# A gated mix of softmax and linear attention on one core: changed order of work, ten P slots, more zero-adding matmuls

## The chip, the cores and the metric

One NeuronCore of a Trainium2 chip runs the whole kernel in one launch. The metric is the device time in microseconds (us); lower is better. Four engines matter: PE (TensorE, matmuls), ACT (ScalarE, the exponentials), DVE (VectorE) and, at the edges, POOL (GpSimd). Transfers are issued by SP and ACT.

## The reference, cut to what matters

```python
x = A_x                                   # [1, 2048, 512] bf16
g = sigmoid((x * gate_w).sum(-1, keepdims=True))
# A: softmax attention, 32 heads of width 16
q, k, v = heads(x @ A_wqkv)
a = merge(softmax(q @ k.T * 16 ** -0.5) @ v) @ A_wo
# B: linear attention, 32 heads of width 16
q, k, v = heads(x @ B_wqkv)
phi = lambda t: where(t > 0, t + 1, exp(t)) + 1e-6
pq, pk = phi(q), phi(k)
b = merge((pq @ (pk.T @ v)) / (pq @ pk.sum(0) + 1e-6)) @ B_wo
return g * a + (1 - g) * b
```

Nearly all of the work is in `softmax(q @ k.T) @ v`: 32 heads of 2048 x 2048 scores, each of which needs an exponential.

## The kernel before, in words

**Rounds.** The attention is cut into 32 rounds (`NR`): a round is one chunk of 512 queries and four heads, one for each quarter of the PE rows. A round has 16 key blocks of 128 keys; a key block has four units, one per head, each a 128 x 512 tile of transposed scores.

**The ACT path.** `emit_act_group` (L809) issues the score matmuls of three or two units, in turn, into PSUM banks 0 to 2 or 3 and 4 (they use 32 rows of PE each and run side by side), and then one exponential on ACT (L826) that reads these banks and writes one slot of `PT`. There are `NPT` = 7 slots. `emit_pv` (L876) multiplies four units of a key block by V into the accumulator, bank 7 (four matmuls with 17 columns each, side by side); a slot is free again when its units have been used. Score matmuls have to wait until ACT has read their banks, and ACT has to wait for a free slot.

**The DVE path.** Of a round's key blocks, the last ones (11 to 15) may be claimed for DVE (`d_claim`, L922). For such a block PE makes the scores one unit at a time in a spare bank, 5 or 6 (`emit_d`, or riding with an ACT group, `d_ride`); DVE turns each into 16-bit integers in `Lb` (`d_s1`, L1002), and a chain of four instructions over the whole block (`chain_op`: L1024, L1027, L1031, L1034) makes two factors `Eb` and `Xb` out of the bits. `emit_dpv` then takes three passes of PE, with `Lb`, `Eb` and `Xb`, into the accumulator. A block of the next round may be claimed ahead of time, as far as the buffers go (three of `Lb` and `Xb`, `NE` = 2 of `Eb`); its passes wait until the accumulator is at its round. For the current round a block is claimed only while

```python
if max(DV.clock, PE.clock) + DLAT > AC.clock + rem * 0.445 + DGRACE:
    continue
```

is false, with `DLAT, DGRACE = 10.5, 2.0` and `rem` the units that the round still has for ACT.

**The end of a round.** When every unit of the round is in the accumulator, `round_end` (L896) transposes it on DVE (L899) and scales it. The next round's PV matmuls need the same bank and wait for L899.

**Everything else** (projections, casts of K, Q and V, the linear attention, the output projection) is cut into tasks, generators that yield one PE or DVE step at a time, in banks 5 and 6. Each task has a due time, by which the tasks are sorted, and a time before which it doesn't start (`nb`), both in rounds. What a round needs and hasn't got is finished on the spot (`need`). V comes in two parts: `V0` for the first eight heads, and `V1`, one task per key block, for the other 24, which are first used in the third round. POOL makes `VX`, a scaled copy of V for blocks 11 to 15.

**The order** is laid out when the program is built. A loop (from L1123 on) keeps a clock for each engine from fixed costs, collects the candidates (0 ACT group, 1 DVE scores, 2 PV, 3 DVE passes, 4 tasks, 5 a chain instruction), and of those that are ready takes the one with the lowest number that ends before the next ACT group has to be issued (`must`). What it emits is each engine's queue, in this order for good. Where nothing fits and the gap on its own clock is long enough, it emits a dummy (`emit_dummy`): four matmuls of zeros, 17 columns each, added to the accumulator, if the accumulator is free by its clock and if the columns that it lately sent through PE (`warm_count`) are under `WARMC`:

```python
if gap > mcost("col", 1) - 0.05 and warm_count() < WARMC and dummy_cand() <= now and apos[0] < NR:
    emit_dummy()
    continue
```

All matmuls are recorded under one helper, L358; tiles tell them apart (scores `sb_QP,sb_KT`, PV `sb_PT,sb_V`, dummies `sb_warm`).

Of the kernel before, what the change touches and what calls it, by code (L numbers as in the profile page):

```python
# [13 lines left out]

STATS = {}
LOG = []
INF = 1e18
SEMLAT = 0.05

# [106 lines left out]
def _ready(E, reads, writes):  # L126
    t = 0.0
    for d in _deps_for(E, reads, writes):
        if d is not None:
            t = max(t, d.t)  # L130
    return t
# [14 lines left out]
def bass_gated_mix__mha_block__linear_attn_block__prompt_kernel(  # L146
# [14 lines left out]
    NTB = S // 128  # L161
# [1 line left out]
    NCC = D // 128  # L163
    SCALE = float(Dh) ** -0.5
    NR = NQC * 8
    NPT = 7
    NL = 3
    NE = 2
    NX = 3
    DKB0 = 11  # L170
    VW = Dh + 1

    with ExitStack() as es:
# [118 lines left out]
        def op(E, fn, reads=(), writes=(), cost=0.2):  # L292
            ev = E.add(fn, _deps_for(E, reads, writes), cost=cost, lag=0.12 if E is AC else 0.0)
            _record(E, ev, reads, writes)
            return ev
# [37 lines left out]
        def mcost(m, waves):  # L333
            return (0.0 if m == mode[0] else 0.095) + 0.015 + 0.2145 * waves

        def pe(fns, reads=(), writes=(), waves=1.0, m="full", cols=None):
            deps = _deps_for(PE, reads, writes)
            n = len(fns)
            first = None
            cost = mcost(m, waves)  # L340
            mode[0] = m
            for k, fn in enumerate(fns):
                ev = PE.add(fn, deps if k == 0 else (), inc=(k == n - 1), cost=cost / n, lag=0.155)
                if k == 0:
                    first = ev
            first.t = ev.t
            c = 512.0 * waves if cols is None else cols
            hist.append((PE.clock, c))
            hsum[0] += c
            for res in reads:  # L350
                res.r[PE] = first
            for res in writes:
                res.w = ev
                res.r = {}
            return ev

        def mm(o, l, r, start=True, stop=True, sg=False):
            return lambda: nc.tensor.matmul(o, lhsT=l, rhs=r, start=start, stop=stop, skip_group_check=sg)  # L358
# [297 lines left out]
        bykey = {}  # L656
        MISCB = [6, 5]
        maxhold = [2]
        DLAT, DGRACE = 10.5, 2.0
        WARMC = 3550.0  # L660

        def add(key, gen, due, nb=-1.0, pre=()):
            t = Task()
            t.pre = list(pre)
            t.key, t.gen, t.due, t.nb, t.seq = key, gen, due, nb, len(bykey)
            t.bank, t.done, t.started = None, False, False
            t.req = next(gen)
            tasks.append(t)
            bykey[key] = t
            tasks.sort(key=lambda k: (k.due, k.seq))  # L670
# [214 lines left out]
            pv_left[r] -= 4  # L885
            round_check()

        def dummy_cand():
            return _ready(PE, (), [r_acc]) + SEMLAT

        def emit_dummy():
            STATS["dummies"] = STATS.get("dummies", 0) + 1
            pe([mm(acc[32 * j:32 * j + VW, :], warm[:, 0:VW], warm, start=False, stop=False, sg=True) for j in range(4)],
               reads=[r_warm], writes=[r_acc], waves=1, m="col", cols=512)

        def round_end(r):  # L896
            qc, t8, par = rinfo(r)
# [24 lines left out]
        def d_claim():  # L922
            r = apos[0]
            if r >= NR or progress() < 0.8:
                return None
            for rr in (r, r + 1):
                if rr >= NR or rr < 1:
                    continue
                kb = NTB - 1 - claimed[rr]
                if kb < DKB0 or act_done[rr]:  # L930
                    continue
                if kb - front[rr] < 1:
                    continue
                if rr == r:
                    rem = 4 * (NTB - claimed[rr] - 1) - apos[1]
                    if max(DV.clock, PE.clock) + DLAT > AC.clock + rem * 0.445 + DGRACE:
                        continue
                return rr, kb
            return None
# [27 lines left out]
        def d_bank():  # L967
            free = [b for b in MISCB if b not in held]
            if not free:
                return None  # L970
            return min(free, key=bank_free)
# [8 lines left out]
            return b, rd, ready  # L980

        def d_ride(js):
            if not d_start() or d_bank() is None:
                return None
            b, rd, ready = d_ready()
            if max(ready, DV.clock - 1.3) > PE.clock + 0.02:
                return None
            for j in dst["cur"]["js"]:
                if j not in js:
                    return j, b, rd  # L990
            return None

        def d_cand():
            if not d_start() or d_bank() is None:
                return None
            b, rd, ready = d_ready()
            return max(ready, DV.clock - 0.5), b, rd

        def d_s1(j, b):
            cu = dst["cur"]  # L1000
            sl = cu["ls"]
            ev = op(DV, lambda: nc.vector.tensor_scalar(Lb[:, sl, 512 * j:512 * (j + 1)], BK[b], S1A, S1B, op0=ALU.mult, op1=ALU.add),  # L1002
                    reads=[r_bk[b]], writes=[r_L[sl]], cost=0.691)
            cu["js"].remove(j)
            if not cu["js"]:
                cu["rdy"][0] = ev.t
                chainq.append(cu)
                dst["cur"] = None
# [66 lines left out]
                add(("Q", 0, 0), t_qproj(0, 0), -0.19, pre=[("xtr", 0)])  # L1075
            add(("V0", t), t_v0(t), 0.25 * t - 0.15, pre=[("xtr", t)])
        for tb in range(NTB):
            add(("V1", tb), t_v1(tb), 1.2 + 0.05 * tb, 0.5 + 0.08 * tb, pre=XT)
        for tb in range(DKB0, NTB):
            add(("VX0", tb), t_vx(0, tb), 0.8, 0.7, pre=[("V0", tb // 4)])  # L1080
            add(("VX1", tb), t_vx(1, tb), 1.9, 1.5, pre=[("V1", tb)])
        add(("gate",), t_gate(), 0.6, 0.5, pre=XT)
        for t8 in range(1, 4):
            for t in range(4):
# [37 lines left out]
        while True:  # L1122
# [21 lines left out]
            if cx is not None:  # L1144
                cands.append((cx[0], 3, mcost("col", 1), emit_dpv, cx))
            for (rt, kind, t, waves) in misc_candidates():
                cands.append((rt, 4, mcost("full", waves) if kind == "pe" else 0.0, lambda c: advance(c[0]), (t,)))
            if chainq:
                cands.append((max(now, DV.clock - 0.3), 5, 0.0, chain_op, None))
            if not cands:  # L1150
                if not tasks and apos[0] >= NR and not pvq and not dpv:
                    break
# [2 lines left out]
                        t.nb = -1  # L1155
                    continue
                raise AssertionError(("stuck", apos, acc_round, len(pvq), [t.key for t in tasks][:5]))
            avail = sorted((c for c in cands if c[0] <= now + 0.02), key=lambda c: c[1])
            pick = None
            for c in avail:  # L1160
                if c[1] == 0 or c[2] == 0.0 or now + c[2] <= must:
# [2 lines left out]
            if pick is None:  # L1164
                pick = cands[0] if avail and act_live else min(cands, key=lambda c: c[0])
                gap = pick[0] - now
                if gap > mcost("col", 1) - 0.05 and warm_count() < WARMC and dummy_cand() <= now and apos[0] < NR:
                    emit_dummy()
                    continue
                if PE.clock < pick[0] < INF:  # L1170
                    PE.clock = pick[0]
# [66 lines left out]
```

## Time and profile before

| | before |
|---|---|
| median of 2 runs | 933.72 us (928.06 and 939.39) |
| profiled execution | 930.83 us, of which the span of the instructions is 929.0 us |
| mean granted TensorE clock | 0.838 |
| ACT busy | 809.3 us (87%) |
| PE busy | 801.4 us (86%) |
| DVE busy | 670.8 us (72%) |
| key blocks taken by DVE | 82 (instructions of L1024) |
| dummies among the rounds | 588 matmuls, in fours 147 |

Two runs 11 us apart are all that the median rests on. In the rows below, a group of instructions reads: line, engine, operation, output<-inputs, shapes, count | busy time in us, mean ns of one | idle time of the engine just before them, and what ended it. A line of the timeline reads: start, duration, engine, line, operation, count, and in brackets the idle time before it and what ended it. A line of a table by stretches reads: the stretch, its length, then busy us and count of instructions for PE, PEld, DVE, ACT and POOL, the granted TensorE clock (1.00 is 2.4 GHz, 0.50 is 1.2 GHz), the DMA share and GB/s; where a tile is chosen, of the instructions of that tile alone, and only the engines that have any. In a row of waits stand the total in us, how often, and the longest.

### The profile page before, as it was taken

The page shows a single profiled execution, that of the slowest core. Times are in us where ns is not written, and L with a number is a line of the kernel's source. Part 1 is how long each engine was busy: PE and PEld are TensorE (multiplying, and loading weights), DVE is VectorE, ACT ScalarE, POOL GpSimd, SP SyncE. Part 2 cuts the span into 40 slices and gives each one's busy share as a digit, 9 for nine tenths or more (in the row PEclk, how much of TensorE's full clock was granted, in tenths as well). Part 3 has the DMA queues.
Part 4 walks back from the last instruction along what each step waited for, and adds up shares of the span by engine and source line. Part 5 has one row for each costly group of instructions (what it writes and reads, how often), then busy time and mean ns, then how long its engine had stood idle before and what let it go on. Part 6 is the DMA issues. An engine that isn't in the chain of part 4 may idle for free.

```text
span 929.0 us, 14661 instructions
## 1 busy us (share of the span) xinstructions
PE 801.4 (86%) x6228; PEld 203.3 (22%) x6228; DVE 670.8 (72%) x1001; ACT 809.3 (87%) x723; POOL 16.6 (2%) x43
## 2 busy tenths in 40 slices
PE   5897898888888889898988888988898979988898
PEld 2322222211121112222112222222222222222112
DVE  3257778878777877856657888768667767878983
ACT  3995989999898978989978999979997979979994
POOL 2103000000000000000000000000000000000000
PEclk9989889979687867789757999997788789977856
DMA  9000000000000000101001000000000000000000
GB/s 215 1 7 1 7 1 5 2 1 7 1 7 1 3 5 1 30 1 52 1 1 52 1 7 9 23 22 1 18 24 12 11 16 26 7 8 18 6 1 23
DMA packets 30769, 14.72 MB, mean 16 GB/s; under 512 B 18544, under 2 KB 30704, under 8 KB 30704
## 3 DMA queue, kind: packets, MB, share of 16 engines
q1 hardware_dynamic: 26512, 11.95, 4.9%
q10 hardware_dynamic: 4192, 1.84, 1.0%
q8 instruction: 49, 0.80, 0.3%
q14 instruction: 16, 0.13, 0.0%
HBM read 6.55 MB, written 2.10 MB: 9 GB/s over the span
## 4 chain that ended last, share of the span: by engine, by line
ACT 56%; PE 34%; DVE 7%; issue 2%; DMA 1%; ACTq 0%; DVEq 0%
ACT sb_PT L826 54%; PE ps L358 34%; DVE sb_Lb L1002 2%; ACT sb_ebuf L528 1%; DMA sb_OT<-in_A_wqkv_dram 1%; DVE sb_Xb L1034 1%; DVE sb_Xb L1031 1%; DVE sb_U L899 1%; DVE sb_Eb L1027 0%; DVE sb_wA L646 0%; DVE sb_xnat L532 0%; DVE sb_Xb L1024 0%; DVE sb_ebuf L530 0%; DVE sb_V L495 0%; DVE sb_phiK L532 0%
## 5 line engine op out<-in xcount | busy, mean ns | idle before, releaser
L826 ACT ACTIVATE sb_PT<-ps 128x1536 bf16<-128x1536 f32 (+1 forms) x688 | 796.9, 1306 | 93.9 <-PE ps L358 91.9
L358 PE MATMUL ps<-sb_QP,sb_KT 32*128 32x512 bf16 x2048 | 357.6, 444 | 84.5 <-ACT sb_PT L826 73.6
L1002 DVE TENSOR_SCALAR sb_Lb<-ps 128x512 uint16<-128x512 f32 x328 | 222.3, 688 | 162.1 <-PE ps L358 160.7
L358 PE MATMUL ps<-sb_PT,sb_V 128*17 128x512 bf16 x1720 | 192.6, 449 | 10.1 <-DVE sb_U L899 8.5
L358 PEld LDWEIGHTS ps<-sb_QP,sb_KT 32*128 32x128 bf16 x2048 | 79.1, 93 | 381.8 <-ACT sb_PT L826 263.1
L1034 DVE TENSOR_TENSOR sb_Xb<-sb_Xb,sb_Lb 128x2048 bf16<-128x2048 bf16 x82 | 100.3, 1223 | 2.4
L1031 DVE TENSOR_TENSOR sb_Xb<-sb_Xb 128x2048 bf16<-128x2048 bf16 x82 | 99.8, 1217 | 0.0
L358 PEld LDWEIGHTS ps<-sb_PT,sb_V 128*17 128x17 bf16 x1720 | 40.7, 89 | 143.9 <-issue 120.0
L358 PE MATMUL ps<-sb_warm 128*17 128x512 bf16 (+1 forms) x596 | 63.9, 466 | 1.3 <-POOL sb_dummy L382 1.3
L1027 DVE TENSOR_SCALAR sb_Eb<-sb_Lb 128x2048 uint16<-128x2048 uint16 x82 | 56.2, 685 | 0.0
L1024 DVE TENSOR_SCALAR sb_Xb<-sb_Lb 128x2048 uint16<-128x2048 uint16 x82 | 56.0, 683 | 0.0
L358 PE MATMUL ps<-sb_Xb,sb_VX 128*17 128x512 bf16 x328 | 38.0, 453 | 11.1 <-DVE sb_Xb L1034 10.9
L358 PE MATMUL ps<-sb_Lb,sb_V 128*17 128x512 bf16 x328 | 39.1, 473 | 6.0 <-DVE sb_Lb L1002 5.2
L358 PE MATMUL ps<-sb_Eb,sb_V 128*17 128x512 bf16 x328 | 38.0, 453 | 2.4 <-DVE sb_Eb L1027 2.2
L358 PE MATMUL ps<-sb_xT,sb_wA 128*128 128x512 bf16 x108 | 31.4, 398 | 0.7 <-DVE sb_Lb L1002 0.5
L899 DVE STREAM_TRANSPOSE sb_U<-ps 128x512 f32<-128x512 f32 x32 | 22.7, 710 | 11.2 <-PE ps L358 10.5
L358 PE MATMUL ps<-sb_wBx,sb_xT 128*128 128x512 bf16 x64 | 24.9, 492 | 0.0
L528 ACT ACTIVATE sb_ebuf<-ps 128x512 f32<-128x512 f32 x32 | 21.4, 669 | 3.0 <-PE ps L358 3.0
L446 DVE CAST sb_KT<-ps 128x512 bf16<-128x512 f32 x16 | 11.0, 688 | 18.0 <-PE ps L358 17.9
L358 PE MATMUL ps<-sb_phiK,sb_xnat 128*128 128x512 bf16 x64 | 22.6, 458 | 0.2 <-DVE sb_Lb L1002 0.2
L646 DVE CAST sb_wA<-ps 128x512 bf16<-128x512 f32 x16 | 10.9, 688 | 16.1 <-PE ps L358 16.1
L358 PE MATMUL ps<-sb_phiK 128*128 128x512 bf16 x64 | 21.5, 439 | 0.0
(78 smaller groups left out, 324.7 us busy)
## 6 DMA issues: line engine op xcount, KB each, us to landing
out_dram<-sb_wA SPq DMA_DIRECT2D x16, 128.0 KB, 1.7
sb_QP<-sb_QT SPq DMA_DIRECT2D x120, 16.0 KB, 1.8
sb_xnat<-in_A_x_dram ACTq DMA_DIRECT2D x2, 512.0 KB, 5.6
sb_wA<-in_A_wqkv_dram SPq DMA_DIRECT2D x2, 512.0 KB, 7.0
sb_wBx<-in_B_wqkv_dram SPq DMA_DIRECT2D x2, 512.0 KB, 6.0
sb_xnat<-in_A_x_dram SPq DMA_DIRECT2D x2, 512.0 KB, 4.0
sb_phiK<-sb_wA SPq DMA_TRANSPOSE x64, 2.2
sb_wA<-in_A_wqkv_dram ACTq DMA_DIRECT2D x1, 512.0 KB, 5.8
```

The costliest lines, as they stand in the source:

```text
L358: return lambda: nc.tensor.matmul(o, lhsT=l, rhs=r, start=start, stop=stop, skip_group_check=sg)
L446: op(DV, lambda: nc.vector.tensor_copy(KT[:, t8, 512 * t:512 * (t + 1)], BK[b]), reads=[r_bk[b]], writes=[r_KT[t8][t]], cost=0.69)
L528: op(AC, lambda: nc.scalar.activation(ebuf[:, s, :], BK[b], ACT.Exp), reads=[r_bk[b]], writes=[r_e[s]], cost=0.68)
L646: op(DV, lambda: nc.vector.tensor_copy(outt[:, sl, :], BK[b]), reads=[r_bk[b]], writes=[r_outt[sl], r_wA[2]], cost=0.69)
L826: op(AC, lambda: nc.scalar.activation(PT[:, slot, 0:512 * n], ps[:, 512 * set_[0]:512 * (set_[0] + n)], ACT.Exp, scale=SCALE), reads=wr, w ...
L899: op(DV, lambda: nc.vector.transpose(U[:], acc), reads=[r_acc], writes=[r_U], cost=0.69)
L1002: ev = op(DV, lambda: nc.vector.tensor_scalar(Lb[:, sl, 512 * j:512 * (j + 1)], BK[b], S1A, S1B, op0=ALU.mult, op1=ALU.add), reads=[r_bk[b ...
L1024: ev = op(DV, lambda: nc.vector.tensor_scalar(X, L, 0x7F, 0x3F80, op0=ALU.bitwise_and, op1=ALU.bitwise_or), reads=[rl], writes=[rx], cost= ...
L1027: ev = op(DV, lambda: nc.vector.tensor_scalar(E_, L, 0xFF80, None, op0=ALU.bitwise_and), reads=[rl], writes=[re_], cost=CH[1])
L1031: ev = op(DV, lambda: nc.vector.tensor_tensor(xb, xb, xb, ALU.mult), reads=[rx], writes=[rx], cost=CH[2])
L1034: ev = op(DV, lambda: nc.vector.tensor_tensor(xb, xb, lb, ALU.mult), reads=[rx, rl], writes=[rx], cost=CH[3])
```

## The change: what it does

- **Claims.** `DLAT` is now a factor of 1.3 on the DVE work still ahead (the chains in the queue, 2.8 for the block's scores and 3.8 for its chain, in the planner's costs), and `DGRACE` is 4.0. With an empty queue the allowance is 1.3 x 6.6 - 4.0 = 4.6 where it was 10.5 - 2.0 = 8.5; with a whole chain in the queue it is 9.5. `NE` is 3.
- **A round's last block first.** `d_urgent` is true when the block at the head of the chain queue belongs to a round that ACT has left or is about to leave. Then no scores of a later round's block are started, and the chain is offered earlier. Chain instructions now rank ahead of the paid PE work (0.5 or 0.6 in place of 5), DVE steps of tasks ahead of everything (-1), and `d_s1` puts a chain instruction ahead of a score conversion for which DVE would have to wait.
- **P slots.** `NPT` is 10.
- **Like with like.** Among what is ready, PE work in the mode PE is in (row, column, full) comes first.
- **Zero-adding matmuls.** `WARMC` is 5200. `warm_mm` takes the place of `emit_dummy`; where the accumulator isn't free by the planner's clock (a round's end), it sends one full-size matmul of zeros to a free spare bank.
- **V1** goes from key block 15 down to 0 and starts and falls due earlier; `VX1` likewise.

A list for statistics (`COLS`) costs the chip nothing and is left out here.

```diff
--- before.py
+++ after.py
@@ -163,9 +164,9 @@
     NCC = D // 128
     SCALE = float(Dh) ** -0.5
     NR = NQC * 8
-    NPT = 7
+    NPT = 10
     NL = 3
-    NE = 2
+    NE = 3
     NX = 3
     DKB0 = 11
     VW = Dh + 1
@@ -656,8 +658,8 @@
         bykey = {}
         MISCB = [6, 5]
         maxhold = [2]
-        DLAT, DGRACE = 10.5, 2.0
-        WARMC = 3550.0
+        DLAT, DGRACE = 1.3, 4.0
+        WARMC = 5200.0
 
         def add(key, gen, due, nb=-1.0, pre=()):
             t = Task()
@@ -885,13 +887,20 @@
             pv_left[r] -= 4
             round_check()
 
-        def dummy_cand():
-            return _ready(PE, (), [r_acc]) + SEMLAT
-
-        def emit_dummy():
-            STATS["dummies"] = STATS.get("dummies", 0) + 1
-            pe([mm(acc[32 * j:32 * j + VW, :], warm[:, 0:VW], warm, start=False, stop=False, sg=True) for j in range(4)],
-               reads=[r_warm], writes=[r_acc], waves=1, m="col", cols=512)
+        def warm_mm(gap):
+            if apos[0] >= NR or warm_count() >= WARMC:
+                return False
+            now = PE.clock
+            if gap > mcost("col", 1) - 0.05 and _ready(PE, (), [r_acc]) + SEMLAT <= now:
+                pe([mm(acc[32 * j:32 * j + VW, :], warm[:, 0:VW], warm, start=False, stop=False, sg=True) for j in range(4)],
+                   reads=[r_warm], writes=[r_acc], waves=1, m="col", cols=512)
+                return True
+            if gap > mcost("full", 1) - 0.05:
+                for b in MISCB:
+                    if b not in held and bank_free(b) + SEMLAT <= now:
+                        pe([mm(BK[b], warm[:, 0:128], warm)], reads=[r_warm], writes=[r_bk[b]], waves=1)
+                        return True
+            return False
 
         def round_end(r):
             qc, t8, par = rinfo(r)
@@ -933,7 +942,8 @@
                     continue
                 if rr == r:
                     rem = 4 * (NTB - claimed[rr] - 1) - apos[1]
-                    if max(DV.clock, PE.clock) + DLAT > AC.clock + rem * 0.445 + DGRACE:
+                    back = sum(sum(CH[c["ck"]:]) for c in chainq) + 2.8 + sum(CH)
+                    if max(DV.clock, PE.clock) + DLAT * back > AC.clock + rem * 0.445 + DGRACE:
                         continue
                 return rr, kb
             return None
@@ -980,6 +990,8 @@
             return b, rd, ready
 
         def d_ride(js):
+            if d_urgent() and (dst["cur"] is None or dst["cur"]["r"] > chainq[0]["r"]):
+                return None
             if not d_start() or d_bank() is None:
                 return None
             b, rd, ready = d_ready()
@@ -990,7 +1002,15 @@
                     return j, b, rd
             return None
 
+        def d_urgent():
+            if not chainq:
+                return False
+            r = chainq[0]["r"]
+            return r < apos[0] or (4 * (NTB - claimed[r]) - apos[1]) * 0.445 + AC.clock < PE.clock + 6.0
+
         def d_cand():
+            if d_urgent() and (dst["cur"] is None or dst["cur"]["r"] > chainq[0]["r"]):
+                return None
             if not d_start() or d_bank() is None:
                 return None
             b, rd, ready = d_ready()
@@ -999,6 +1019,8 @@
         def d_s1(j, b):
             cu = dst["cur"]
             sl = cu["ls"]
+            if chainq and DV.clock < r_bk[b].w.t - 0.1:
+                chain_op()
             ev = op(DV, lambda: nc.vector.tensor_scalar(Lb[:, sl, 512 * j:512 * (j + 1)], BK[b], S1A, S1B, op0=ALU.mult, op1=ALU.add),
                     reads=[r_bk[b]], writes=[r_L[sl]], cost=0.691)
             cu["js"].remove(j)
@@ -1075,10 +1097,10 @@
                 add(("Q", 0, 0), t_qproj(0, 0), -0.19, pre=[("xtr", 0)])
             add(("V0", t), t_v0(t), 0.25 * t - 0.15, pre=[("xtr", t)])
         for tb in range(NTB):
-            add(("V1", tb), t_v1(tb), 1.2 + 0.05 * tb, 0.5 + 0.08 * tb, pre=XT)
+            add(("V1", tb), t_v1(tb), 0.9 + 0.05 * (15 - tb), 0.45 + 0.06 * (15 - tb), pre=XT)
         for tb in range(DKB0, NTB):
             add(("VX0", tb), t_vx(0, tb), 0.8, 0.7, pre=[("V0", tb // 4)])
-            add(("VX1", tb), t_vx(1, tb), 1.9, 1.5, pre=[("V1", tb)])
+            add(("VX1", tb), t_vx(1, tb), 1.7 - 0.1 * (tb - DKB0), 0.5, pre=[("V1", tb)])
         add(("gate",), t_gate(), 0.6, 0.5, pre=XT)
         for t8 in range(1, 4):
             for t in range(4):
@@ -1144,9 +1166,12 @@
             if cx is not None:
                 cands.append((cx[0], 3, mcost("col", 1), emit_dpv, cx))
             for (rt, kind, t, waves) in misc_candidates():
-                cands.append((rt, 4, mcost("full", waves) if kind == "pe" else 0.0, lambda c: advance(c[0]), (t,)))
+                cands.append((rt, 4 if kind == "pe" else -1, mcost("full", waves) if kind == "pe" else 0.0, lambda c: advance(c[0]), (t,)))
             if chainq:
-                cands.append((max(now, DV.clock - 0.3), 5, 0.0, chain_op, None))
+                if d_urgent():
+                    cands.append((max(now, DV.clock - 1.0), 0.5, 0.0, chain_op, None))
+                else:
+                    cands.append((max(now, DV.clock - 0.3), 0.6, 0.0, chain_op, None))
             if not cands:
                 if not tasks and apos[0] >= NR and not pvq and not dpv:
                     break
@@ -1155,7 +1180,9 @@
                         t.nb = -1
                     continue
                 raise AssertionError(("stuck", apos, acc_round, len(pvq), [t.key for t in tasks][:5]))
-            avail = sorted((c for c in cands if c[0] <= now + 0.02), key=lambda c: c[1])
+            pmode = {0: "row", 1: "row", 2: "col", 3: "col", 4: "full"}
+            avail = sorted((c for c in cands if c[0] <= now + 0.02),
+                           key=lambda c: (c[1] > 0 and c[2] > 0, c[1] if c[1] <= 0.6 else 1 if pmode[c[1]] == mode[0] else 2, c[1]))
             pick = None
             for c in avail:
                 if c[1] == 0 or c[2] == 0.0 or now + c[2] <= must:
@@ -1164,8 +1191,7 @@
             if pick is None:
                 pick = cands[0] if avail and act_live else min(cands, key=lambda c: c[0])
                 gap = pick[0] - now
-                if gap > mcost("col", 1) - 0.05 and warm_count() < WARMC and dummy_cand() <= now and apos[0] < NR:
-                    emit_dummy()
+                if warm_mm(gap):
                     continue
                 if PE.clock < pick[0] < INF:
                     PE.clock = pick[0]
```

## Rows read from the trace of the kernel before

**Rows 1.** The page, parts 1 and 2: busy time, granted clock in 40 slices.

```profile
PE 801.4 (86%) x6228; PEld 203.3 (22%) x6228; DVE 670.8 (72%) x1001; ACT 809.3 (87%) x723; POOL 16.6 (2%) x43
...
PEclk9989889979687867789757999997788789977856
```

**Rows 2.** The page, part 4: the chain that ended last, by engine.

```profile
ACT 56%; PE 34%; DVE 7%; issue 2%; DMA 1%; ACTq 0%; DVEq 0%
```

**Rows 3.** Waits, whole span: who waited for whom.

```profile
DVE sb_Lb L1002 <- PE ps L358: 160.7, 188, 4.3
ACT sb_PT L826 <- PE ps L358: 91.9, 88, 11.7
```

**Rows 4.** Groups by line, whole span.

```profile
L826 ACT ACTIVATE sb_PT<-ps 128x1536 bf16<-128x1536 f32 (+1 forms) x688 | 796.9, 1306 | 93.9 <-PE ps L358 91.9
...
L1002 DVE TENSOR_SCALAR sb_Lb<-ps 128x512 uint16<-128x512 f32 x328 | 222.3, 688 | 162.1 <-PE ps L358 160.7
...
L1034 DVE TENSOR_TENSOR sb_Xb<-sb_Xb,sb_Lb 128x2048 bf16<-128x2048 bf16 x82 | 100.3, 1223 | 2.4
...
L1024 DVE TENSOR_SCALAR sb_Xb<-sb_Lb 128x2048 uint16<-128x2048 uint16 x82 | 56.0, 683 | 0.0
```

**Rows 5.** Table of the 33 stretches at the lower granted clock: one, and their sum.

```profile
729.40:749.90 20.50, 20.50 (x146) 4.92 (x146) 12.67 (x19) 17.60 (x15) 0.00 (x0) 0.50 0.05 10
...
sum 300.20, PE 289.56 PEld 56.30 DVE 196.53 ACT 238.10 POOL 2.57; mean PE 8.77 PEld 1.71 DVE 5.96 ACT 7.22 POOL 0.08
```

**Rows 6.** Table of the 34 stretches at the upper granted clock: their sum.

```profile
sum 612.80, PE 503.73 PEld 143.88 DVE 470.04 ACT 569.70 POOL 8.51; mean PE 14.82 PEld 4.23 DVE 13.82 ACT 16.76 POOL 0.25
```

**Rows 7.** Groups on PE, 729.4 to 749.9, lower clock: PV matmuls.

```profile
L358 PE MATMUL ps<-sb_PT,sb_V 128*17 128x512 bf16 x36 | 5.5, 596 | 0.0
```

**Rows 8.** Groups on PE, 522.5 to 551.6, upper clock: PV matmuls.

```profile
L358 PE MATMUL ps<-sb_PT,sb_V 128*17 128x512 bf16 x60 | 5.7, 384 | 0.0
```

**Rows 9.** Table of three stretches at the upper clock, each round a round's end.

```profile
87.50:91.10 3.60, 2.07 (x12) 0.57 (x10) 3.60 (x6) 0.00 (x0) 3.60 (x4) 1.00 0.00 0
762.90:766.50 3.60, 0.86 (x11) 0.29 (x11) 3.47 (x6) 0.00 (x0) 0.00 (x0) 1.00 0.05 10
609.90:613.50 3.60, 2.10 (x30) 0.62 (x29) 3.60 (x6) 1.32 (x2) 0.00 (x0) 1.00 0.11 36
```

**Rows 10.** The same table for the dummies (sb_warm) alone, last stretch.

```profile
609.90:613.50 3.60, 1.43 (x24) 0.51 (x24) 0.00 (x0) 1.00 0.11 36
```

**Rows 11.** Timeline of ACT at rounds' ends: first, one and last of eight.

```profile
94.09 1.02 ACT L826 ACTIVATE sb_PT<-ps 128x1024 bf16<-128x1024 f32 x1 [11.69 <-PE ps L358]
...
617.06 1.45 ACT L826 ACTIVATE sb_PT<-ps 128x1536 bf16<-128x1536 f32 x1 [5.83 <-PE ps L358]
...
821.17 1.45 ACT L826 ACTIVATE sb_PT<-ps 128x1536 bf16<-128x1536 f32 x1 [3.78 <-PE ps L358]
```

**Rows 12.** Timeline, 610 to 616: DVE up to the round's end.

```profile
610.74 0.68 DVE L1002 TENSOR_SCALAR sb_Lb<-ps 128x512 uint16<-128x512 f32 x1
...
615.53 0.71 DVE L899 STREAM_TRANSPOSE sb_U<-ps 128x512 f32<-128x512 f32 x1
```

**Rows 13.** Timeline, 82 to 94: one of four rows of V casts there.

```profile
85.88 1.15 DVE L495 CAST sb_V<-ps 128x384 bf16<-128x384 f32 x2
```

**Rows 14.** Timeline of ACT, 905 to 929: its last exponentials.

```profile
914.59 2.36 ACT L826 ACTIVATE sb_PT<-ps 128x1536 bf16<-128x1536 f32 x2 [0.91 <-PE ps L358]
```

**Rows 15.** Groups on PE, whole span, shapes kept apart: the dummies.

```profile
L358 PE MATMUL ps<-sb_warm 128*17 128x512 bf16 x588 | 60.3, 464 | 0.0
```

**Rows 16.** Timeline of PE, 603 to 612: passes in changing and in one mode.

```profile
603.84 0.39 PE L358 MATMUL ps<-sb_QP,sb_KT 32*128 32x512 bf16 x3
604.16 0.40 PE L358 MATMUL ps<-sb_PT,sb_V 128*17 128x512 bf16 x4
...
610.60 0.83 PE L358 MATMUL ps<-sb_warm 128*17 128x512 bf16 x12
```

**Rows 17.** The 33 stretches at the lower clock, the dummies (sb_warm) alone: sum.

```profile
sum 300.20, PE 28.84 PEld 4.88 POOL 0.00; mean PE 0.87 PEld 0.15 POOL 0.00
```

More of the change, by code (lines that the diff above doesn't have):

```diff
@@ L16 @@
 LOG = []
+COLS = []
 INF = 1e18
@@ L348, in pe @@
             hist.append((PE.clock, c))
+            COLS.append((PE.clock, c))
             hsum[0] += c
```

## The prediction, made before the kernel was run

> **What bounds the kernel now.** I read the page first: ACT and PE are both busy for some 87% of the span, DVE for 72%, and the granted clock is anything from 0.6 to 1.0 in the 40 slices [rows 1]. The chain that ended last runs 56% through ACT and 34% through PE [rows 2]. So two regimes take turns: in one ACT is late, in the other PE. The waits give the same in us: ACT's exponentials waited 91.9 us for score matmuls [rows 3]. Whatever isn't in those waits is work of ACT itself, 796.9 us in exponentials [rows 4], or the ends of the run.
>
> To part the regimes I cut the span at the changes of the granted clock and let the table add up each kind. At 0.50, which is 1.2 GHz, the kernel spends 300.2 us in 33 stretches, and there PE is busy for 289.6 us, 96%: PE is the bound, ACT idles 300.2 - 238.1 = 62.1 us, and DVE 103.7 us [rows 5]. At 1.00, 2.4 GHz, 612.8 us, PE is busy for 503.7 us only and ACT idles 612.8 - 569.7 = 43.1 us [rows 6]. A quarter of the PE passes show why: four PV matmuls side by side last 596 ns each at the lower level and 384 ns at the upper [rows 7, 8], 0.21 us more for the same pass. The chip lowers the clock after PE has had thin stretches: two rounds' ends where PE was busy for 2.07 and 0.86 of 3.60 us were both still at 1.00, and lower stretches, two of the 33, follow within half a us, while none follows on a third, busy for 2.10 us [rows 9]. In that third one 24 of the 30 matmuls were dummies, in the other two there were none [rows 10]. So zero-adding matmuls count as work for the clock, as far as one pair of stretches can say it.
>
> The second loss stands at the rounds' ends. When ACT has filled all P slots and the accumulator isn't free, ACT stops. Eight times it did so for over 2 us within a few us of a round's end: 11.69, 2.35, 3.13, 3.13, 5.83, 4.56, 4.46 and 3.78, in all 38.9 us [rows 11]. One of them in detail: the last block's last score conversion on DVE starts at 610.74, its chain follows, and the round's transpose comes at 615.53 [rows 12]; ACT stands from 611.2 to 617.06. The longest one, at 82.4, is of another make: V1 was needed at once and its casts sat on DVE between the steps of the round's last block [rows 13].
>
> **The change, part by part.** The sum is made against the profiled execution, 930.8 us (span 929.0 and 1.8 around it); the median of the two runs, 933.7, is 2.9 above it, and I add that at the end.
>
> *More zero-adding matmuls, like with like.* They touch the 62.1 us that ACT idles at the lower clock. Of these 12.3 us are rounds' ends, counted below (2.35 + 3.13 + 3.78, and the 3.0 of the 11.69 that lie behind 91.1), and 3.7 us lie behind the last exponential, which ends at 916.95 in a stretch that ends at 920.6 [rows 14]. That leaves 46.1 us as the price of the lower clock. PE idles 612.8 - 503.7 = 109 us at the upper clock; the trace shows 147 dummy passes now [rows 15], and the old limit leaves many gaps open. A dummy between two passes of another mode takes some 0.32 us of PE's time (a pass of scores starts at 603.84 and the PV pass behind it at 604.16), one among its like 0.215 (three take 0.83 us with 0.40 for the last) [rows 16], so some 340 more would fit in the 109 us at most; gaps under 0.27 us by the planner's clock stay open, and I take 150. Bounds: nothing is won if the planner's gaps don't lie where the chip's are (the planner counts at full clock and knows nothing of the lower level); all 46.1 if the clock stays up. I take two thirds, **-31**, since the gaps before a fall are mostly waits for ACT, which the planner sees, and since a clock that stays up also brings the chip nearer to the plan.
>
> What the fillers cost: nothing at the upper clock as long as the gap is there. Behind each waits the next score group, and behind that ACT. A pass takes 0.215 + 0.21 = 0.43 us at the lower level, where PE has no gaps; of the dummies' busy time now, 60.3 us, 28.8 lie there, about half [rows 15, 17]. With a third of the lower time left, a sixth of 150 passes, 25 x 0.43 = 11 us, lands there, and half of it reaches ACT: **+5**. Bounds 0 and the slower rival below.
>
> The Trainium skill, TensorEngine Tiling (Array Packing), section Key Properties, speaks against the fillers: a change of the tiling mode drains TensorE. The trace agrees, with a step of 0.32 - 0.215 = 0.11 us for a change of mode [rows 16]. If all 150 fillers cost two such steps that ACT feels, that is 33 us; it is a rival below.
>
> *Ten P slots, the last block first, V1 earlier.* A slot is 796.9/688 = 1.16 us of ACT [rows 4], so three more let ACT run on for 3.5 us at each stop: 11.69 becomes 8.2, 5.83, 4.56, 4.46 and 3.78 become 2.3, 1.1, 1.0 and 0.3, and the three others vanish, a gain of 26 us. V1 in descending order and earlier should take off more of the 11.69, and a chain that isn't held up by later scores brings L899 forward. Against it stands the new rule for claims: with an empty queue a block may be claimed 8.5 - 4.6 = 3.9 us (by the planner's clock) nearer to the round's end, which is as much as the three slots cover. Bounds: all 38.9 gained, or as much lost. I take half, **-19**. What the earlier chain is moved past: PE's paid work of the planner's list, which it doesn't delay, and the next block's L1002, for which PE has spare banks 5 and 6 to hold; what is late then is the next block's scores, and nobody needs those before the next round's end. POOL's copies VX come earlier with V1 and lie beside work of the first rounds. Each step's transfers stay as they are: no DMA is added, and the queue of SP has the same issues.
>
> *More blocks on DVE.* A block takes DVE 4 x 0.68 + 2 x 0.68 + 2 x 1.22 = 6.5 us (L1024 and L1034 stand for their twins) and spares ACT four units, 1.6 groups of 2.5 on average, 1.85 us [rows 4]. DVE waited 160.7 us for scores [rows 3], at most 24 blocks; a third `Eb` lets one more block be taken ahead at each round's end, and the claims are looser with an empty queue, tighter by 1 us with a full one, and shut while a chain is urgent. Bounds: 5 blocks fewer (+9) to 20 more (-37); I take 6 more, **-11**. On PE a block takes three passes for one and up to four single scores for one shared pass, five more of 0.32 us or so, 1.6 us, hidden at the upper clock where PE has 18% to spare.
>
> Sum: 930.8 - 31 + 5 - 19 - 11 = 874.8, and with the 2.9 us to the median **878**.
>
> **The rivals.** (a) *The clock stays up nearly throughout*: -46 and no filler felt, -26 at the rounds' ends, and 12 blocks, -22: 933.7 - 94 = 840. For it: at the upper clock ACT is busy for 569.7 of 612.8 us, 93%, with stops and ends of the run in it [rows 6]. Against it: 33 falls in the present plan show how far the chip's gaps stray from it. (b) *The clock doesn't gain, slots and claims do*: 933.7 - 19 - 11 = 904. (c) *The fillers' drains are felt*, the mechanism of 0.11 us twice for each of 150, 33 us in place of 5: 906. (d) *DVE becomes late*: with blocks claimed later and more of them the stops at the rounds' ends double, +39 in place of -19; with the clock's gain and the claims 933.7 + 39 - 31 + 5 - 11 = 936. For it: at the upper clock DVE is busy for 470.0 of 612.8 us already [rows 6], and a stop needs only one late conversion. Against: the P slots cover the first 3.5 us. (e) *Slower: the fillers feed the lower clock.* If the falls stay, half of the 150 passes land where PE has no gap, 75 x 0.43 = 32 us on the path that ends last, and rounds' ends, fed by the same PE, gain nothing: 966. It decides when the lower clock keeps more than some 0.6 of its 300 us, since 46 x (1 - s) is then less than 32 x s. For it: PE is 96% busy there already. Against: a lower stretch ends after dense PE work, and dummies make it denser than single scores do.
>
> **How the numbers follow.** Chances: my forecast 0.49, (a) 0.18, (b) 0.09, (c) 0.06, (d) 0.10, (e) 0.08. The likeliest is my sum, 878, with 855 to 900 as its own range. For 8 in 10 I leave out the upper half of (d), (e) and the lower end of (a): 838 to 925. About 2% is what a measurement of this kernel can tell from no change, here 915 and 952: faster takes the forecast, (a) and most of (b) and (c), 0.79; the same the rest of these and (d), 0.13; slower (e), 0.08.
>
> **What would show it.** The granted clock in the mean: 0.93 or so for 0.838, with a lower total near 100 us. Dummies: about 300 passes for 147, some of them full-size. ACT's waits on PE: near 45 us for 91.9; stops over 2 us at rounds' ends: three or four for eight, and none of 11 us at the end of the second round. L1024: 88 for 82, and ACT busy for about 798 us. DVE's wait for scores falls below 120 us. I am wrong if the mean clock stays under 0.88, which (b) and (e) share and the sum of the fillers' time at 0.50 tells apart; if L899 comes later behind ACT's last exponential of a round, which is (d); or if more dummies leave ACT's waits at 90 us with the clock up, which is (c).

## The result and the profile after

The changed kernel takes 826.9 us (median of 824.8 and 829.0) for 933.7; the ratio is 0.886, with a 95% interval of 0.861 to 0.911. That is faster, as forecast, and more so: 51 us under the forecast and 11 us under the lower end of the range. The profiled execution took 829.0 us for 930.8. An execution more than 1.5% above the fastest of its kernel counts as slow and enters no comparison; the only one is the profiled execution of experiment 4.

Of the page after, the busy times, the granted clock in 40 slices and the chain that ended last by engine, which answer to [rows 1, 2]:

```profile
PE 749.2 (91%) x7077; PEld 212.3 (26%) x7077; DVE 698.1 (84%) x1041; ACT 788.0 (95%) x715; POOL 15.5 (2%) x43
...
PEclk8977999999999999999999999999999999999999
...
ACT 84%; PE 10%; DVE 3%; DMA 2%; issue 1%; ACTq 0%
```

There is one regime left: ACT is busy for 95% of the span and the chain runs 84% through it. From the fifth slice on the clock is at 0.9 or more. Of the table by stretches, one of the four at the lower clock and their sum, which answer to [rows 5]:

```profile
53.60:70.70 17.10, 16.46 (x73) 2.85 (x73) 7.91 (x14) 10.62 (x9) 3.65 (x3) 0.50 0.01 3
...
sum 30.70, PE 26.55 PEld 5.29 DVE 14.71 ACT 18.28 POOL 3.65; mean PE 6.64 PEld 1.32 DVE 3.68 ACT 4.57 POOL 0.91
```

300.2 us at 1.2 GHz have become 30.7, and most of these are one stretch in the second round, in which PE is busy for 16.46 of 17.10 us, some 7 of them with projections. Waits, as in [rows 3]:

```profile
DVE sb_Lb L1024 <- PE ps L360: 66.5, 124, 2.8
...
ACT sb_PT L828 <- PE ps L360: 16.4, 16, 5.5
```

ACT waited 16 times for PE where it had waited 88 times. The chain in order of time shows what became of the rounds' ends [rows 11]; these are two of its pieces (start, duration, what):

```profile
339.50 114.69 ACT sb_PT L828 x102
...
718.10 91.75 ACT sb_PT L828 x81
```

102 exponentials follow one another without a break, over five rounds' ends. No stop over 2 us stands at any round's end; the longest after the start, 2.37 us, lies in the stretch at the lower clock. By groups, as in [rows 4, 15] (the last two rows are of the table that keeps shapes apart):

```profile
L828 ACT ACTIVATE sb_PT<-ps 128x1536 bf16<-128x1536 f32 (+1 forms) x680 | 781.5, 1431 | 16.6 <-PE ps L360 16.4
...
L1049 DVE TENSOR_SCALAR sb_Eb<-sb_Lb 128x2048 uint16<-128x2048 uint16 x87 | 59.5, 684 | 0.0
```

```profile
L360 PE MATMUL ps<-sb_warm 128*17 128x512 bf16 x1356 | 112.9, 386 | 0.0
...
L360 PE MATMUL ps<-sb_warm 128*128 128x512 bf16 x49 | 16.4, 425 | 1.3 <-POOL sb_dummy L384 1.3
```

DVE has 87 blocks for 82. The dummies are 339 column passes and 41 full-size ones (eight of the 49 stand ahead of the rounds) for 147.

**Where the time went.** The span is ACT's busy time and its idle time. Idle fell from 929.0 - 809.3 = 119.7 us to 826.9 - 788.0 = 38.9, by 80.8, nearly all of it the waits for PE (75.5 less). Busy fell by 21.3. Together that is the 102.1 us by which the spans differ. Of the 21.3, eight groups fewer at 1.12 us are 9 (102 exponentials in a row take 114.69 us). The rest is a term that I hadn't seen. An exponential that starts when ACT is at rest takes 1.45 or 1.02 us (three or two units) [rows 11], but one of each in a row takes 2.36 and not 2.47 [rows 14]: the second starts before the first has ended, and the two overlap by 0.11 us. (The Trainium skill, ScalarE: Activation LUTs, section What ACT_TABLE_LOAD costs, gives some 0.09 us for each pair; the 0.11 measured here is used.) Counted in the two traces, 122 of the 688 exponentials before start with ACT at rest, and 21 of the 680 after. These 101 at 0.11 are 11 us; with the groups that is 20 of the 21.3.

### The profile page after: what moved, and what is told of

Read it like the earlier page. It is cut to its first block, busy times and chain, and to the rows that moved or that the text cites. A ratio compares the mean times of both kernels' runs of the same rounds, so it can differ in the third digit from the quotient of the medians.

```text
span 826.9 us, 16440 instructions
## 1 busy us (share of the span) xinstructions
PE 749.2 (91%) x7077; PEld 212.3 (26%) x7077; DVE 698.1 (84%) x1041; ACT 788.0 (95%) x715; POOL 15.5 (2%) x43
## 4 chain that ended last, share of the span: by engine, by line
ACT 84%; PE 10%; DVE 3%; DMA 2%; issue 1%; ACTq 0%
ACT sb_PT L828 82%; PE ps L360 10%; ACT sb_ebuf L530 2%; DMA sb_OT<-in_A_wqkv_dram 1%; DMA sb_wA<-in_A_wqkv_dram 1%; DVE sb_Lb L1024 1%; DVE sb_gT L522 0%; DVE sb_Xb L1053 0%; DVE sb_U L908 0%; DVE sb_Xb L1046 0%; ACTq L304 0%; DVE sb_KT L448 0%; DVE sb_Xb L1056 0%; DVE sb_Eb L1049 0%; DVE sb_V L497 0%
## 5 line engine op out<-in xcount | busy, mean ns | idle before, releaser
L828 ACT ACTIVATE sb_PT<-ps 128x1536 bf16<-128x1536 f32 (+1 forms) x680 | 781.5, 1431 | 16.6 <-PE ps L360 16.4
L360 PE MATMUL ps<-sb_QP,sb_KT 32*128 32x512 bf16 x2048 | 313.3, 389 | 54.4 <-ACT sb_PT L828 42.9
L1024 DVE TENSOR_SCALAR sb_Lb<-ps 128x512 uint16<-128x512 f32 x348 | 234.6, 687 | 69.4 <-PE ps L360 66.5
L360 PE MATMUL ps<-sb_PT,sb_V 128*17 128x512 bf16 x1700 | 168.5, 389 | 2.3 <-DVE sb_U L908 1.1
L360 PE MATMUL ps<-sb_warm 128*17 128x512 bf16 (+1 forms) x1405 | 129.3, 387 | 1.3 <-POOL sb_dummy L384 1.3
L1056 DVE TENSOR_TENSOR sb_Xb<-sb_Xb,sb_Lb 128x2048 bf16<-128x2048 bf16 x87 | 106.2, 1221 | 1.9
L1053 DVE TENSOR_TENSOR sb_Xb<-sb_Xb 128x2048 bf16<-128x2048 bf16 x87 | 105.8, 1216 | 0.0
L360 PEld LDWEIGHTS ps<-sb_warm 128*17 128x17 bf16 (+1 forms) x1405 | 33.4, 90 | 38.6 <-issue 25.1
L360 PE MATMUL ps<-sb_wA,sb_xT 128*128 128x128 bf16 (+1 forms) x128 | 20.6, 287 | 2.9 <-DVE sb_V L497 1.7
L360 PE MATMUL ps<-sb_xT,sb_wBx 128*128 128x512 bf16 x64 | 18.3, 384 | 0.3 <-DVE sb_Lb L1024 0.3
```

The lines of the kernel that those rows point to most:

```text
L828: op(AC, lambda: nc.scalar.activation(PT[:, slot, 0:512 * n], ps[:, 512 * set_[0]:512 * (set_[0] + n)], ACT.Exp, scale=SCALE), reads=wr, w ...
L1053: ev = op(DV, lambda: nc.vector.tensor_tensor(xb, xb, xb, ALU.mult), reads=[rx], writes=[rx], cost=CH[2])
L1056: ev = op(DV, lambda: nc.vector.tensor_tensor(xb, xb, lb, ALU.mult), reads=[rx, rl], writes=[rx], cost=CH[3])
```

## The experiments

Each kernel was timed in three rounds against the kernel before on its chip, whose median was 925 to 930 us there; times are medians. The changed kernel wasn't timed again with them: differences to it are to the 826.9 us of two executions, and those of 10 us or less aren't settled. "Fillers" are the zero-adding matmuls, a "stop" is an idle time of ACT of over 2 us. "Lower clock" is the total of the stretches at 1.2 GHz.

**1. The fillers taken back.** Edits in the changed kernel:

```diff
-        WARMC = 5200.0
+        WARMC = 3550.0
...
-            if gap > mcost("full", 1) - 0.05:
+            if False:
```

> The changed kernel with the old limit (3550) and without full-size fillers; all else as changed. Theory A (the added fillers hold the clock, and that is most of the gain): mean granted clock near 0.87, over 150 us at the lower clock, 880 to 905 us. Theory B (claims, order and slots bring the chip's gaps to where the planner put its dummies, and the clock follows): clock over 0.95, 827 to 845 us.

870.3 us, ratio 0.940 (0.933 to 0.946), clock 0.861. The busy times, the sum of its 22 stretches at the lower clock, and ACT's wait:

```profile
PE 760.4 (87%) x6132; PEld 196.3 (23%) x6132; DVE 695.8 (80%) x1033; ACT 800.0 (92%) x717; POOL 16.4 (2%) x43
```

```profile
sum 242.30, PE 233.12 PEld 45.38 DVE 177.66 ACT 198.18 POOL 6.24; mean PE 10.60 PEld 2.06 DVE 8.08 ACT 9.01 POOL 0.28
```

```profile
ACT sb_PT L828 <- PE ps L360: 46.4, 78, 5.0
```

Neither theory. The clock is as A has it, so claims, order and slots don't hold it up; but the time lies 10 us under A's range, so they bring over 50 us with 242.3 us still at the lower clock for 300.2. At the lower clock ACT idles 242.3 - 198.2 = 44.1 us here. In the whole span of 870.9 us it idles 70.9, 32.0 more than in the changed kernel, and it is busy for 12.0 more.

**2. The fillers alone**, in the kernel before: `warm_mm` with its limit of 5200 in the place of `emit_dummy`, nothing else.

> The kernel before with the new limit (5200) and the full-size fillers; order, claims, V1 and seven slots as before. Theory A: clock over 0.95, ACT's waits on PE from 92 down to 45 us or less, mostly stops at rounds' ends, 865 to 885 us. Theory B: clock under 0.90, 910 to 930 us.

879.6 us, ratio 0.950 (0.943 to 0.956), clock 0.965: A's time and clock. ACT still waits 57.4 us for PE, more than A had it, and six stops over 3 us stand at rounds' ends, with a seventh of 2.42 they are 35.45 us for 38.9 before. The busy times, and three of the stops in the timeline of ACT:

```profile
PE 786.1 (90%) x7398; PEld 221.9 (25%) x7398; DVE 676.6 (77%) x1009; ACT 796.5 (91%) x722; POOL 18.4 (2%) x43
```

```profile
97.69 1.02 ACT L826 ACTIVATE sb_PT<-ps 128x1024 bf16<-128x1024 f32 x1 [8.51 <-PE ps L358]
```

```profile
379.36 1.45 ACT L826 ACTIVATE sb_PT<-ps 128x1536 bf16<-128x1536 f32 x1 [7.20 <-PE ps L358]
```

```profile
642.09 1.02 ACT L826 ACTIVATE sb_PT<-ps 128x1024 bf16<-128x1024 f32 x1 [5.13 <-PE ps L358]
```

So the stops aren't a matter of the clock. ACT's idle time fell by 119.7 - 81.2 = 38.5 us (span 877.7) and its busy time by 12.8. DVE's wait for scores fell too, from 160.7 to 93.9, and yet only one block came with it (83):

```profile
DVE sb_Lb L1009 <- PE ps L358: 93.9, 148, 4.7
```

**3. Seven slots.** `NPT = 7` in the changed kernel.

> The changed kernel with seven P slots. If the slots cover stops at rounds' ends as the prediction had it (3.5 us each): stops over 2 us come back, 15 to 25 us in all, 842 to 855 us. If urgent chains and a held clock had already removed the stops: under 833 us.

833.3 us, ratio 0.902 (0.896 to 0.909), and no stop over 2 us at a round's end. It is at the edge of the second case: the stops are gone without the slots. The 6 us to the changed kernel lie within the intervals.

**4. No fillers at all.** `WARMC = 0.0` in the changed kernel.

> The changed kernel with no zero-adding matmul among the rounds at all. Theory A: clock under 0.80, 915 to 960 us, slower than with the old fillers. Theory B: clock over 0.92 and 830 to 855 us.

887.6 us (three executions of 882 to 892), ratio 0.959 (0.952 to 0.967), clock 0.770 to 0.785. The profile is of a longer execution, 900.6 us with a clock of 0.744, and shows the kind of loss rather than its size. Its 32 stretches at the lower clock in sum, and ACT's wait:

```profile
sum 460.90, PE 440.88 PEld 86.47 DVE 349.84 ACT 390.56 POOL 6.05; mean PE 13.78 PEld 2.70 DVE 10.93 ACT 12.20 POOL 0.19
```

```profile
ACT sb_PT L828 <- PE ps L360: 62.4, 94, 4.9
```

The clock falls as A says, under that of the kernel before (0.831 to 0.855 on this chip); the time doesn't follow A's 915 to 960: with no dummy at all the new order is still 37 us faster than the old one with its dummies. What the old order takes without dummies, no run shows.

**5. The chain's part taken back**: no `d_urgent`, no chain ahead of a late conversion, and the chain last again.

```diff
-            if d_urgent() and (dst["cur"] is None or dst["cur"]["r"] > chainq[0]["r"]):
-                return None
...
-            if chainq and DV.clock < r_bk[b].w.t - 0.1:
-                chain_op()
...
-                if d_urgent():
-                    cands.append((max(now, DV.clock - 1.0), 0.5, 0.0, chain_op, None))
-                else:
-                    cands.append((max(now, DV.clock - 0.3), 0.6, 0.0, chain_op, None))
+                cands.append((max(now, DV.clock - 0.3), 5, 0.0, chain_op, None))
```

(The sort key is changed with it, so that rank 5 stands behind the paid work.)

> The changed kernel without d_urgent and without the chain's higher rank (chain instructions last again, later rounds' scores not held back, no chain instruction ahead of a late conversion). Theory C (the stops at rounds' ends were late chains, and finishing the last block first is what removes them): stops over 2 us come back at five or more rounds' ends, 850 to 870 us. Theory D (claims, V1 and like with like had removed them): no such stops, under 835 us.

855.0 us, ratio 0.919 (0.914 to 0.923): C's time, but by another way than C's. One stop is back, at the end of the second round, and ten blocks are lost; the stop, the exponentials, the blocks and DVE's wait for scores:

```profile
95.31 2.36 ACT L828 ACTIVATE sb_PT<-ps 128x1536 bf16<-128x1536 f32 x2 [8.50 <-PE ps L360]
```

```profile
L828 ACT ACTIVATE sb_PT<-ps 128x1536 bf16<-128x1536 f32 (+1 forms) x696 | 799.2, 1423 | 23.0 <-PE ps L360 22.9
...
L1043 DVE TENSOR_SCALAR sb_Eb<-sb_Lb 128x2048 uint16<-128x2048 uint16 x77 | 52.8, 686 | 0.0
```

```profile
DVE sb_Lb L1018 <- PE ps L360: 88.4, 150, 5.0
```

77 blocks for 87 are 16 groups more on ACT, whose exponentials took 799.2 - 781.5 = 17.7 us more; its waits on PE took 22.9 - 16.4 = 6.5 more. The spans of the two profiled executions differ by 23.7, so that is all of it. The chain's part is what fills DVE.

**6. Without like with like.** The sort in the changed kernel looks at rank alone.

```diff
-  key=lambda c: (c[1] > 0 and c[2] > 0, c[1] if c[1] <= 0.6 else 1 if pmode[c[1]] == mode[0] else 2, c[1])
+  key=lambda c: (c[1] > 0 and c[2] > 0, c[1])
```

> The changed kernel without putting PE work of the present mode first. If changes of mode take PE time that matters: PE's waits behind ACT stay, mean clock under 0.97, 840 us or more. If the 0.11 us of a change is hidden at the upper clock: 824 to 832 us.

836.8 us, ratio 0.899 (0.894 to 0.904), clock 0.961: between the two cases. It may be worth one per cent; the intervals don't settle it.

**7. The old V1 order.** The four due and starting times of V1 and VX1 as before.

> The changed kernel with V1 and VX1 in their old order and at their old times. If this is what removed the long stop at the end of the second round: a stop of 6 to 12 us is back there, 833 to 840 us. If finishing the block first does it: 825 to 830 us.

835.0 us, ratio 0.897 (0.891 to 0.904). The time fits the first case, the trace doesn't: no long stop at the end of the second round; the longest wait behind the start is 2.74 us, in the middle of that round.

```profile
72.22 15.93 ACT L828 ACTIVATE sb_PT<-ps 128x1536 bf16<-128x1536 f32 x14 [2.74 <-PE ps L360]
```

The time is 8 us above the changed kernel's, which doesn't settle what V1 is worth; but V1's order isn't what removed the 11.69 us.

**8. The old claims.** `DLAT, DGRACE = 10.5, 2.0`, added rather than multiplied, and `NE = 2`.

> The changed kernel with the old claim rule (10.5 and 2.0) and two Eb buffers. If the claims bring blocks: 80 to 83 blocks for 87, ACT busy for 795 us or more, 833 to 842 us. If the held clock and the order bring them: 85 or more blocks and under 832 us.

830.9 us, ratio 0.894 (0.889 to 0.900), with as many blocks as the changed kernel:

```profile
L1049 DVE TENSOR_SCALAR sb_Eb<-sb_Lb 128x2048 uint16<-128x2048 uint16 x87 | 59.5, 684 | 0.0
```

The second case holds: the claims bring no block.

**9. The chain's part alone**, in the kernel before: the lines of experiment 5 put in, and the rank of -1 for DVE steps of tasks.

> The kernel before with the chain's part alone: d_urgent, the chain's and the DVE steps' higher ranks, a chain instruction ahead of a late conversion. Old dummies, seven slots, old claims, two Eb, old V1. If this part by itself finishes the rounds' ends and feeds DVE: 86 or more blocks for 82, no stop over 2 us at a round's end after the third round, clock still under 0.88, 870 to 885 us. If it needs slots, claims and V1 beside it: stops stay, 900 us or more.

867.9 us, ratio 0.936 (0.931 to 0.941), clock 0.877: the first case, 2 us under its range. The blocks, the two waits, and the sum of its 21 stretches at the lower clock:

```profile
L1039 DVE TENSOR_SCALAR sb_Eb<-sb_Lb 128x2048 uint16<-128x2048 uint16 x87 | 60.2, 692 | 0.0
```

```profile
DVE sb_Lb L1014 <- PE ps L358: 93.8, 158, 2.1
...
ACT sb_PT L826 <- PE ps L358: 40.8, 56, 4.8
```

```profile
sum 211.60, PE 203.79 PEld 40.56 DVE 150.17 ACT 169.97 POOL 1.53; mean PE 9.70 PEld 1.93 DVE 7.15 ACT 8.09 POOL 0.07
```

By itself it brings all five blocks, ends every stop over 2 us at a round's end, and, with 100 dummy passes for 147, leaves 89 us fewer at the lower clock.

**10. The fillers and the chain's part together**, in the kernel before.

> The kernel before with two parts, the fillers and the chain's part. If these two carry the gain: 828 to 842 us, clock over 0.96, ACT's waits on PE under 25 us. If slots, claims, V1 and like with like matter together though each alone gives little: 845 us or more.

833.0 us, ratio 0.899 (0.892 to 0.905), ACT's waits on PE 24.1 us, the profiled execution's clock 0.957, just under the 0.96 expected. These two parts carry the gain. The ratios of 9 and 2, each alone, multiply to 0.936 x 0.950 = 0.889, near the 0.899 here and the changed kernel's 0.886.

**11. Late chains and seven slots**: experiment 5 with `NPT = 7`.

> The changed kernel without the chain's part and with seven slots. Where chains are late, three more slots should be worth 3.5 us at each stop, as the prediction had it: stops over 2 us come back at five or more rounds' ends, 15 us or more above the 855.0 us of the same kernel with ten slots. If slots do nothing here either: within 5 us of it.

864.7 us, ratio 0.934 (0.929 to 0.939), 9.7 us above experiment 5, though it has 81 blocks to 77 (four blocks are 7.4 us of ACT). That is less than the 15 us expected, and four stops for five or more, but not nothing either. Four stops over 2 us, of which two in the timeline of ACT:

```profile
94.66 1.02 ACT L828 ACTIVATE sb_PT<-ps 128x1024 bf16<-128x1024 f32 x1 [11.01 <-PE ps L360]
```

```profile
400.80 1.02 ACT L828 ACTIVATE sb_PT<-ps 128x1024 bf16<-128x1024 f32 x1 [4.80 <-PE ps L360]
```

The others are 5.05 and 3.48. With ten slots the first is 8.50 and the rest are gone. ACT's waits on PE are 34.1 us for 22.9, 2.8 for each of the four. So where chains are late the slots do about what the prediction gave them; where chains are in time there is nothing to cover.

**12. Fillers without a limit.** `WARMC = 1e9` in the changed kernel.

> The changed kernel with no limit on the fillers: one in every gap that the planner finds long enough. If a filler's change of mode or its pass is felt by ACT: ACT's waits grow by some 0.1 us for each added pass, 835 us or more. If gaps hide them: within 4 us of the changed kernel, 823 to 831 us.

824.5 us, ratio 0.889 (0.885 to 0.894), clock 0.987. The dummies, as above, and ACT's wait:

```profile
L360 PE MATMUL ps<-sb_warm 128*17 128x512 bf16 x1868 | 150.4, 381 | 0.0
...
L360 PE MATMUL ps<-sb_warm 128*128 128x512 bf16 x65 | 21.5, 421 | 1.3 <-POOL sb_dummy L384 1.3
```

```profile
ACT sb_PT L828 <- PE ps L360: 12.9, 15, 5.8
```

144 passes more than the changed kernel cost nothing that ACT feels. It beats the kernel before beyond doubt; over the changed kernel its lead of 2 us can't be told from none.

## Why the prediction was wrong

**What was right.** The bound, its two regimes and both mechanisms: fillers hold the clock (experiments 1, 2 and 4), and stops at rounds' ends come from the last block's late chain (5, 9 and 11). That holds for the longest one, too, for which the prediction blamed V1's casts: with V1 as before it is gone where the chain's part is in (7, 9), and with V1 moved it is back where the part is out, 8.50 and 11.01 us (5, 11). The blocks, 87 for the 88 that I gave.

**The step that failed** is the term for the rounds' ends, "Ten P slots, the last block first, V1 earlier", and with it that for the blocks. I priced the slots by rows, gave the chain's part one clause without a number ("a chain that isn't held up by later scores brings L899 forward"), set against both a loss by the new claims, and took half: -19. The runs show another picture. The chain's part alone ends all the stops, 38.9 us in the trace of before. The slots are idle cover beside it (experiment 3), though 3.5 us apiece was about right where they are needed (11). The claims neither lose nor win (8). And the blocks that I had from the claims, six forecast and five measured, come from the chain's part (5, 9), which by itself makes the kernel 6.4% faster. That I looked for its effect at the rounds' ends only is the error of reading. DVE's wait for scores [rows 3] was a row to look at for it: it went from 160.7 to 93.8 us in experiment 9. But that row alone doesn't give the blocks, since the fillers alone bring it to 93.9 with one block more (2). Which of the lines of the chain's part does it (the hold on later scores, the higher ranks, the chain ahead of a late conversion), no run takes apart.

**The clock's term was of the right kind and too small.** ACT's idle time fell by 80.8 us, of which 38.9 are the stops; the other 41.9 stand against -31, with a price of 46.1. By the medians the fillers are worth 43 us in the changed kernel (1) and 45 in the old one (2). That looks like the whole price, but only 32.0 and 38.5 us of it (the latter with 3.5 of stops) are idle time, which is what the price counts; 12.0 and 12.8 are ACT's busy time (a block's 1.9 in each): with the clock up, ACT's exponentials more often start before the one ahead has ended (572 of 682 in experiment 1, 659 of 680 in the changed kernel; 566 of 688 before, 656 of 687 in experiment 2). For that the term had nothing. The +5 for fillers that ACT feels was nothing (12).

**ACT's own work** fell by 21.3 us and not by 11: 9 are the groups, as the price of a block had it, and 11 the exponentials that no longer start alone, which the sum put at nothing.

**Together.** The sum had 874.8 us for the profiled execution, which took 829.0. Of these 46 us, 20 are the rounds' ends, 11 the clock, 10 ACT's own work and 5 the cost of fillers.

**The range.** Rival (a) was the right one and had 840. With the bounds that the text itself named, 46.1 and 38.9, and the 21.3 of ACT's work, it would have been 933.7 - 106.3 = 827.4. That this all but meets the median is partly luck: the spans differ by 102.1, and the 21.3 is known only now. I put the range's lower end at (a) although (a) took 26 of the 38.9, the slots' part only.

**The other rivals.** (b), no gain from the clock, falls by experiment 1 against the changed kernel, and by 2. (d), DVE late, falls: DVE is busy for 84%, and no stop follows from it. (e) falls: 30.7 us are left at the lower clock. (c), drains that ACT feels, was the rule of the Trainium skill, TensorEngine Tiling (Array Packing), section Key Properties, that a change of tiling mode drains TensorE. The step of 0.11 us in [rows 16] stands, but 144 more passes in experiment 12 leave ACT's waits at 12.9 us for 16.4: in a gap the drain is hidden, and the measurement decides against a cost here.

**What stays open**: whether slots, V1, claims and like with like are worth anything together. Each taken back costs 4 to 10 us at the median, the four left out at once 6 (10), and the intervals are as wide.

## What to carry to other kernels

When ACT or DVE is the bound and PE waits on it, cheap matmuls in PE's gaps can pay for themselves through the clock. Read their worth off the engine's idle time in the stretches at the lower clock, of which most came back here, and add what the engine's own instructions save when they follow one another without a break. A change of priorities deserves a term of its own, priced at the waits that it can fill, and not only at the place it is named for. When the bounds of two independent terms are both mechanisms with rows behind them, the range has to reach to their sum.

## What the runs showed of the hardware that I had not expected

The lower clock is cheap for a kernel that ACT bounds: with 242.3 us at 1.2 GHz experiment 1's profiled execution takes 872.7 us for 829.0 with 30.7, some 0.21 us for each us at half speed. That the clock follows PE's activity is how the Trainium skill puts it, too (TensorE: Matmul & The Clock Gate, Part 1: throttled by default, released by activity); experiment 4 with 0.770 to 0.785 and experiment 12 with 0.987, the same rules of order with no dummy and with 524 passes, agree, and show that zeros count as activity. And an engine that is let run costs less itself: ACT was busy for 21.3 us less, of which the eight groups that are gone explain 9 and the 0.11 us of overlap between exponentials in a row 11.
